# A gated window attention: w_q loaded in two pieces, wo's first piece in halves around the last values, three blocks ahead of the parts' sum

## The chip, the core and the metric

The kernel runs on one core of a Trainium2 chip. The core has a matrix engine (TensorE, PE in the profile; its weight loads are listed as PEld), a vector engine (VectorE, DVE), a scalar engine (ScalarE, ACT), GpSimd (POOL) and SyncE (SP), which here only issues DMAs. Each engine works through its own instructions in order and waits on semaphores. Sixteen DMA engines carry the transfers; every large transfer is spread over all of them. The metric is the device time of one execution in microseconds, the median of the runs shown.

## The reference

Two tokens (batch 2, one position, D = 512) are normalised and go through two branches. What is computed, cut to what matters:

```python
xn = layernorm(x)                                   # (2, 1, 512)
# A: attention, 32 query heads, 8 key/value heads of 128, over the last W = 4096 positions
q = xn @ wq                                         # wq (512, 4096)
k, v = k_cache[:, :, -W:], v_cache[:, :, -W:]       # (2, 8, 4096, 128), float32
p = softmax(q k^T * 128**-0.5);  o = p v
s = o.reshape(2, 1, 4096) @ wo                      # wo (4096, 512)
# B: a gated MLP
z = gelu(xn @ w_in)                                 # w_in (512, 1792)
z1, z2 = z[..., :896], layernorm(z[..., 896:])
y = (z1 * (w_sp * z2 + b_sp)) @ w_out               # w_out (896, 512)
out = x + s * silu(y)
```

All is float32. The data to read are some 89 MB: keys and values 33.5 MB each, wq and wo 8.4 MB each, w_in 3.7 and w_out 1.8 MB.

## The kernel before

The large loads all go through SyncE's queue, in this order: win and wout (the MLP's weights), wq in a piece of 4 MB and two of 2 MB (lines 126 to 131), and then the keys K:u and values V:u of eight units u, 4 MB each, and wo. A unit is one batch row and two key/value heads (`load`, line 146). These loads share a ring of four 4 MB slots (line 105, `slot`): win, the two halves of wq, K:0, K:1, V:0, K:2, V:1 and so on take the slots in turn, so that each load is issued when the last reader of the slot's previous content is done. For a K that reader is VectorE's transposition, for a V it is TensorE. xs, the two rows of x, comes over ScalarE's queue (line 119).

The head of the kernel normalises x (`bn_stats`, line 186), turns it (xnT), multiplies win (z, line 240), and runs the MLP between the pieces of wq; `queries(k)` (line 257) multiplies the k-th quarter of wq, and quarters 2 and 3 lie in wq's second half. The order is queries(0), queries(1), the product with wout (y), its copy, queries(2), y_sum, queries(3). Then the queries are spread into qb (`place_queries`, step q).

The rest follows ORDER (line 27), a list of steps written out by hand. Every engine issues its instructions in the order in which the steps stand there (`InOrder`, line 55). For unit u: T:u.0 to T:u.7 transpose the keys on VectorE; shares, keep and scores multiply them with the queries (TensorE, ScalarE, TensorE); rowmax, mg, shmax and bias form the maximum; exp on ScalarE; probs_t transposes the probabilities on VectorE; pv:u.0 and pv:u.1 multiply with the values; lsum, shsum and weights give the softmax denominators; evac copies the result with its weight; col and gather collect it into one of three sets: heads 0 to 3 of both batch rows (units 0, 1, 4, 5), heads 4 and 5 (units 2, 6), heads 6 and 7 (units 3, 7). `spread` (TensorE) and `place` (step oT, VectorE) bring a set into the layout in which it is multiplied with wo.

wo is 32 blocks of 128 rows: 16 for the first set, 8 each for the second and the third. `load_wo(0)` (line 508) loads the first 16 in one piece of 4 MB. `load_wo(1)` loads, into the next slot, the 8 of the second set in one piece and the 8 of the third set in pieces of 4, 2, 1 and 1. `wo_early` (line 520) multiplies 28 blocks, all but the last four: steps X:0.0 to X:0.7 (two blocks each) for the first set, Y:0.0 to Y:0.3 for the second, U:0.0 and U:0.1 for the third. Block after block goes to the next of four groups of 32 rows of one PSUM bank, `part`; step parts copies it to SBUF on ScalarE and step pz (`add_parts`, line 549) sums the four groups into the bank `so`. The last four blocks are multiplied by `wo_last` (line 538) straight into `so`, 8 multiplies each (four groups, and two passes for float32): Z:0 takes the piece of two blocks, Z:1 and Z:2 one block each. The order at the end is Z:0, pz, Z:1, Z:2. Then VectorE multiplies with the gate, adds x and the result is stored (lines 601 to 604).

PSUM banks are handed out by tag: `part` has the tag s0, that of the scores of a unit's first half; acc, the product with the values, has two banks with the tag acc.

Of the kernel before, what the change touches and what calls it, by code (L numbers as in the profile page):

```python
# [9 lines left out]
F32 = mybir.dt.float32  # L10
# [4 lines left out]
P = 128  # L15
# [28 lines left out]
scores:5.1 evac:4 col:4 rowmax:5.0  # L44
K:7 V:6 T:6.0 rowmax:5.1 mg:5 T:6.1 T:6.2 shmax:5 bias:5 T:6.3 exp:5.0 T:6.4 exp:5.1 T:6.5 probs_t:5.0 shares:6.0
keep:6.0 lsum:5 shsum:5 scores:6.0 probs_t:5.1 T:6.6 T:6.7 rowmax:6.0 pv:5.0 weights:5 shares:6.1 keep:6.1 pv:5.1
V:7 T:7.0 wo:0 scores:6.1 rowmax:6.1 T:7.1 T:7.2 mg:6 T:7.3 shmax:6 bias:6 T:7.4 evac:5 col:5 exp:6.0 exp:6.1 T:7.5
probs_t:6.0 T:7.6 T:7.7 wo:1 lsum:6 shares:7.0 keep:7.0 pv:6.0 scores:7.0 shares:7.1 rowmax:7.0 keep:7.1 shsum:6
scores:7.1 probs_t:6.1 weights:6 rowmax:7.1 mg:7 pv:6.1 evac:6 shmax:7 gather:5 col:6 bias:7 exp:7.0 gather:6 exp:7.1
probs_t:7.0 spread:0 probs_t:7.1 lsum:7 spread:1 pv:7.0 shsum:7 oT:0 weights:7 pv:7.1 X:0.6 X:0.0 oT:1 X:0.2 X:0.4  # L50
evac:7 X:0.3 col:7 X:0.7 gather:7 spread:2 X:0.5 Y:0.1 Y:0.0 Y:0.3 X:0.1 Y:0.2 oT:2 U:0.0 U:0.1 parts:0 Z:0 pz:0 Z:1 Z:2
"""


# [16 lines left out]
def kernel(  # L71
# [14 lines left out]
    pe, dve, act, sp = (InOrder(tc, e) for e in (nc.tensor, nc.vector, nc.scalar, nc.sync))  # L86
    B, _, D = x.shape
# [21 lines left out]
    ps = ctx.enter_context(tc.tile_pool(name="ps", bufs=1, space=bass.MemoryType.PSUM))  # L109

    def slot(name, *shape):
        return ring.tile([P, *shape], F32, tag="slot", name=name)

    def bank(name, *shape):
        return ps.tile([P, *shape], F32, tag="kt", name=name, bufs=2)


    xs = sb.tile([B, D], F32, tag="ss", name="xs", bufs=1)
    act.dma_start(xs, x[:, 0, :])
    win_v = w_in.rearrange("(p k) f -> p k f", p=P)  # L120
    win = slot("win", KT, F)
    sp.dma_start(win, win_v)
# [2 lines left out]
    wq_v = wq.rearrange("(p k) f -> p k f", p=P)  # L125
    wqt = []
    for a in range(0, KT, 2):
        t = slot(f"wq{a}", 2, HQ * DH)
        for k, n in ((0, 2),) if a == 0 else ((0, 1), (1, 1)):
            sp.dma_start(t[:, k : k + n], wq_v[:, a + k : a + k + n, :])  # L130
        wqt += [t[:, 0], t[:, 1]]

    wb1 = cst.tile([1, 2], F32, tag="wb1", name="wb1")
# [12 lines left out]
    def load(u, src, name):  # L146
        t = slot(f"{name}{u}", UJ, DH)
        b, v = divmod(u, HKV // 2)
        first = src[b, 2 * v, SK - W, :]
        of = bass.AP(tensor=src.tensor, offset=first.offset, ap=[[UJ * DH, P // 2], [SK * DH, 2], [1, UJ * DH]])  # L150
        sp.dma_start(t.rearrange("p j d -> p (j d)"), of)
        return t
# [73 lines left out]
    for nj in (8, 16):  # L226
# [3 lines left out]
        at = cst.tile([P, nx], F32, tag=f"at{nj}", name=f"at{nj}")  # L230
# [6 lines left out]
    pz = bank("z", 2, FH // G)  # L237
# [30 lines left out]
    u = cst.tile([P, 2, FT, B], F32, tag="u", name="u")  # L268
# [71 lines left out]
    def place_queries():  # L340
        dve.tensor_tensor(
            free_ap(qb, 16, [[REP, G], [32, NP * G], [1, REP]]), free_ap(qa, 0, [[0, G], [REP, NP * G], [1, REP]]),
            free_ap(grpm, 0, [[1, G], [0, NP * G], [0, REP]]), op=ALU.mult,
        )
# [10 lines left out]
    sets = {}  # L355
    for i, (kv, n, nj) in enumerate(SETS):
        o1 = cst.tile([P, B, 32], F32, tag=f"o1_{i}", name=f"o1_{i}")
        oT = cst.tile([P, nj, 32], F32, tag=f"oT_{i}", name=f"oT_{i}")
# [102 lines left out]
    col = {}  # L461
# [22 lines left out]
    def spread(i):  # L484
        o1, oT, nj = sets[f"oT{i}"]
        pts[i] = bank(f"oT_ps{i}", B, 32)
        pe.matmul(pts[i], perms[nj][0].rearrange("p h a x -> p (h a x)"), o1, start=True, stop=True)

    def place(i):
        _, oT, nj = sets[f"oT{i}"]  # L490
        nx = 32 // nj
        t = sb.tile([P, B, nx, nj], F32, tag="ot", name=f"ot{i}", bufs=1)
        dve.tensor_tensor(
            t, pts[i].rearrange("p b (x j) -> p b x j", x=nx), free_ap(perms[nj][1], 0, [[0, B], [1, nx], [0, nj]]),
            op=ALU.mult,
        )
        dve.tensor_reduce(
            oT[:, :, 0 : 16 * B : 16].rearrange("p j b -> p b j"), t.rearrange("p b x j -> p b j x"), axis=AX.X, op=ALU.add
        )


    wo_s = []
# [2 lines left out]
        wo_s.append(wo[r0:r1, :].rearrange("(p j) d -> p j d", j=nj))  # L505
    blocks = []

    def load_wo(n):
        t = slot(f"wo{n}", 16, D)
        a = 0  # L510
        for i in ((0,), (1, 2))[n]:
            for j, n in (((0, 16),), ((0, 8),), ((0, 4), (4, 2), (6, 1), (7, 1)))[i]:
                sp.dma_start(t[:, a : a + n, :], wo_s[i][:, j : j + n, :])
                blocks.append((t[:, a : a + n, :], sets[f"oT{i}"][1], j))
                a += n

    EARLY = 28
    done = 0
# [1 line left out]
    def wo_early(n, at):  # L520
        nonlocal done
        if done == 0:
            part.append(ps.tile([P, 512], F32, tag="s0", name="part"))
        t, oT, j = blocks[n]
        for a in range(at, at + 2):
            g = done % G
            pe.matmul(
                part[0][32 * g : 32 * g + 32, :], oT[:, j + a, :], t[:, a, :], start=(done < G), stop=(done >= EARLY - G)
            )
            done += 1  # L530

    part = []

    def copy_parts():
        parts.append(sb.tile([P, D], F32, tag="o", name="parts", bufs=1))
        act.activation(parts[0], part[0], AF.Copy)

    def wo_last(n):
        if n == 0:
            so.append(bank("so", DC))  # L540
        t, oT, j = blocks[3 + n]
        for a in range(t.shape[1]):
            for g in range(G):
                pe.matmul(
                    so[0][32 * g : 32 * g + 32, :], oT[:, j + a, :], t[:, a, g * DC : (g + 1) * DC],
                    start=(n == 0 and a == 0), stop=(j + a == oT.shape[1] - 1),
                )

    def add_parts():
        for g in range(G):  # L550
            pe.matmul(
                so[0][32 * g : 32 * g + 32, :], rowm, parts[0][:, g * DC : (g + 1) * DC], start=False, stop=False
            )

    parts, so = [], []
    STEPS = dict(
        T=turn, rowmax=row_max, mg=spread_max, shmax=share_max, bias=bias, exp=probs, probs_t=probs_t, lsum=own_sum,
        shsum=share_sum, weights=weights, shares=shares, keep=keep, scores=scores, pv=pv, evac=evacuate, col=collect,
        gather=gather,
    )  # L560

    def step(name, u, a=()):
        if name == "q":
            place_queries()
        elif name == "K":
            units[u].k = load(u, k_cache, "k")
        elif name == "V":
            units[u].v = load(u, v_cache, "v")
        elif name == "wo":
            load_wo(u)  # L570
        elif name == "spread":
            spread(u)
        elif name == "oT":
            place(u)
        elif name == "X":
            wo_early(0, 2 * a[0])
        elif name == "Y":
            wo_early(1, 2 * a[0])
        elif name == "U":
            wo_early(2, 2 * a[0])  # L580
        elif name == "Z":
            wo_last(u)
        elif name == "parts":
            copy_parts()
        elif name == "pz":
            add_parts()
        else:
            STEPS[name](units[u], *a)
# [6 lines left out]
    for line in ORDER.strip().split("\n"):  # L595
        for name in line.split():
            name, at = name.split(":")
            u, _, a = at.partition(".")
            step(name, int(u), (int(a),) if a else ())
# [33 lines left out]
```

## Time and profile before

| what | us |
|---|---|
| median of 3 runs (216.70 to 216.98) | 216.95 |
| the profiled execution | 216.95 |
| its span, first to last instruction | 215.2 |
| PE busy | 134.8 (63%) |
| DVE busy | 126.3 (59%) |
| ACT busy | 51.3 (24%) |
| DMA, mean rate over the span | 416 GB/s |

The profile is of one execution. Times in its rows are microseconds from the span's start. A row of the timeline gives start, duration, engine, line, operation, output and inputs, shapes and count; several instructions of a kind that follow each other are merged into one row with their count. In brackets stands how long the engine was idle before and what ended that. Nearly all instructions carry line 65, that of the helper that issues them, so they are told apart by the tiles' names. The row of a stretch gives its bounds, its length, the busy time and count of the engines asked for, the granted share of TensorE's clock, the busy share of the 16 DMA engines and their rate in GB/s.

### The profile page before, as it was taken

Reading aid. Unit: us, or ns where it says so; the run is one execution under the profiler, and the core shown is the slowest. Engines: PE = TensorE matmul, PEld = TensorE weight load, DVE = VectorE, ACT = ScalarE, POOL = GpSimd, SP = SyncE. Lnnn points to the kernel's source line nnn. Section 1 sums busy time; section 2 is a strip of 40 time slices with the busy share of each in tenths; the row PEclk is TensorE's granted clock in tenths of the full one; section 3 lists DMA queues with packets and bytes.
Section 4 is the critical chain, followed back from the end, with each engine's and each line's share of the span. In section 5 each row is a group of like instructions: output and inputs, shape, how many; then the busy total and the mean of one; then the engine's idle time right before and its main releaser. Section 6 shows DMA issues by size and latency. Waiting matters only on the chain.

```text
span 215.2 us, 2275 instructions
## 1 busy us (share of the span) xinstructions
PE 134.8 (63%) x872; PEld 42.8 (20%) x872; DVE 126.3 (59%) x217; ACT 51.3 (24%) x128; POOL 4.5 (2%) x17
## 2 busy tenths in 40 slices
PE   0174498305857928944890795299349618987893
PEld 0120222001112211312230231113113211232331
DVE  2604311749599599649917981994599089635111
ACT  5002402200116206023330503151251306142201
POOL 8000000000000000000000000000000000000000
PEclk9999559855599985995898599559859976996999
DMA  7999999999999999999999999999999999999990
GB/s 257 427 439 469 390 420 472 397 463 408 463 408 451 423 414 463 402 458 414 451 417 433 439 414 460 402 463 414 445 426 431 433 408 463 408 463 411 410 382 35
DMA packets 3930, 89.54 MB, mean 416 GB/s; under 512 B 446, under 2 KB 462, under 8 KB 848
## 3 DMA queue, kind: packets, MB, share of 16 engines
q1 hardware_dynamic: 3900, 89.40, 96.9%
q8 instruction: 7, 0.11, 0.2%
q14 instruction: 3, 0.02, 0.0%
q10 hardware_dynamic: 20, 0.01, 0.0%
HBM read 89.40 MB, written 0.00 MB: 416 GB/s over the span
## 4 chain that ended last, share of the span: by engine, by line
DMA 73%; DVE 13%; PE 10%; ACT 2%; SPq 1%; issue 1%; ACTq 0%
DMA k<-in_A_k_cache_dram 42%; DMA wq<-in_A_wq_dram 16%; DMA wo<-in_A_wo_dram 15%; DVE kts L65 10%; PE part L65 4%; PE sh L65 2%; PE acc L65 2%; ACT p L65 1%; DVE pT L65 1%; PE q_ps L65 1%; SPq L65 1%; DVE m L65 1%; PE s L65 1%; PE so L65 0%; DVE nb L65 0%
## 5 line engine op out<-in xcount | busy, mean ns | idle before, releaser
L65 DVE STREAM_TRANSPOSE kts<-k 128x1024 f32<-128x1024 f32 x64 | 75.5, 1218 | 33.0 <-DMA k<-in_A_k_cache_dram 33.0
L65 PE MATMUL sh<-kts,qb 128*32 128x512 f32 x256 | 43.7, 808 | 15.8 <-DVE kts L65 12.4
L65 PE MATMUL acc<-v,pT 128*32 128x512 f32 x256 | 33.6, 641 | 5.5 <-DMA v<-in_A_v_cache_dram 3.1
L65 ACT ACTIVATE p<-s,nb 128x512 f32<-128x512 f32 x32 | 22.5, 732 | 43.8 <-DVE nb L65 43.8
L65 ACT ACTIVATE ss<-sh 128x512 f32<-128x512 f32 x16 | 9.6, 597 | 62.1 <-PE sh L65 62.1
L65 PE MATMUL mo<-mg,joint 128*128 128x16 f32 x16 | 4.4, 355 | 29.2 <-DVE mg L65 29.2
L65 DVE STREAM_TRANSPOSE pT<-p 128x1024 f32<-128x1024 f32 x16 | 19.6, 1225 | 2.3 <-ACT p L65 2.2
L65 PE MATMUL s<-ss,sums 128*128 128x512 f32 x32 | 18.8, 671 | 2.3 <-ACT ss L65 2.3
L65 PEld LDWEIGHTS sh<-kts,qb 128*32 128x32 f32 x256 | 9.0, 130 | 39.1 <-issue 35.4
L65 PEld LDWEIGHTS acc<-v,pT 128*32 128x32 f32 x256 | 10.6, 142 | 29.0 <-issue 23.1
L65 DVE TENSOR_REDUCE m<-s 128x1 f32<-128x512 f32 x16 | 10.8, 673 | 5.3 <-PE s L65 5.2
L65 ACT ACTIVATE o<-acc,wd 128x128 f32<-128x128 f32 x32 | 9.1, 368 | 15.3 <-PE acc L65 15.3
L65 PE MATMUL q_ps<-wq,xnT 128*32 128x512 f32 x64 | 11.1, 789 | 2.6 <-DMA wq<-in_A_wq_dram 2.6
L65 PEld LDWEIGHTS mo<-mg,joint 128*128 128x128 f32 x16 | 3.6, 280 | 32.9 <-DVE mg L65 30.2
L65 PE MATMUL z<-win,xnT 128*32 128x448 f32 x32 | 6.1, 945 | 4.4 <-DMA win<-in_B_w_in_dram 4.4
L65 PE MATMUL part<-wo,oT 128*32 128x512 f32 x56 | 7.7, 596 | 1.0 <-DMA wo<-in_A_wo_dram 0.9
L65 PEld LDWEIGHTS s<-ss,sums 128*128 128x128 f32 x32 | 5.0, 197 | 10.8 <-issue 8.2
L65 ACT ACTIVATION_READ_ACCUMULATOR p<-s,nb 128x1 f32 x32 | 6.4, 200 | 0.0
L65 DVE STREAM_TRANSPOSE zs<-zs 128x448 f32<-128x448 f32 x1 | 0.6, 645 | 9.0 <-ACT zs L65 9.0
L65 ACT ACT_TABLE_LOAD x4 | 5.1, 1283 | 2.6 <-POOL hT L164 2.6
L65 DVE TENSOR_SCALAR gate<-ys 128x128 f32<-128x128 f32 x1 | 0.2, 226 | 8.8 <-ACT ys L65 8.8
L65 PE MATMUL col<-o,selw 128*32 128x128 f32 x64 | 4.0, 301 | 1.9 <-ACT o L65 1.9
(109 smaller groups left out, 63.9 us busy)
## 6 DMA issues: line engine op xcount, KB each, us to landing
k<-in_A_k_cache_dram SPq DMA_DIRECT2D x8, 4096.0 KB, 27.1
v<-in_A_v_cache_dram SPq DMA_DIRECT2D x8, 4096.0 KB, 31.2
wq<-in_A_wq_dram SPq DMA_DIRECT2D x1, 4096.0 KB, 24.2
wq<-in_A_wq_dram SPq DMA_DIRECT2D x2, 2048.0 KB
wo<-in_A_wo_dram SPq DMA_DIRECT2D x1, 4096.0 KB, 32.3
win<-in_B_w_in_dram SPq DMA_DIRECT2D x1, 3584.0 KB, 11.2
wo<-in_A_wo_dram SPq DMA_DIRECT2D x1, 2048.0 KB
wout<-in_B_w_out_dram SPq DMA_DIRECT2D x1, 1792.0 KB, 15.0
```

Source lines behind the costliest of these rows:

```text
L65: return self.tc.keep_in_program_order(call(*args, **kwargs))
```

## The change

Five edits go together.

1. wq's second half is loaded in one issue of 4 MB instead of two of 2 MB.
2. xs is loaded by two issues of one row instead of one issue of two rows.
3. wo's first piece (16 blocks) is loaded in two halves of 8 blocks (2 MB): the first is issued ahead of the last values V:7, the second behind them. wo's slot is thus taken ahead of that of V:7. The steps of the first set change with it: X:0.0 to X:0.3 multiply the first half, X:1.0 to X:1.3 the second. X:0.0 to X:0.3 stand ahead of pv:7.0, the product with the last values; for that gather:5, spread:0 and oT:0, which prepare the first set, move forward. X:1.0 and X:1.1 stand ahead of col:7, X:1.2 and X:1.3 behind it.
4. The third set's blocks come in pieces of 4, 3 and 1 instead of 4, 2, 1 and 1. Z:0 now multiplies three blocks, ahead of pz; Z:1 multiplies the last one; there is no Z:2.
5. `part` takes a bank of the tag acc.

The blocks, multiplies and bytes are the same in all.

```diff
--- before.py
+++ after.py
@@ ORDER @@
-V:7 T:7.0 wo:0 scores:6.1 rowmax:6.1 T:7.1 T:7.2 mg:6 T:7.3 shmax:6 bias:6 T:7.4 evac:5 col:5 exp:6.0 exp:6.1 T:7.5
-probs_t:6.0 T:7.6 T:7.7 wo:1 lsum:6 shares:7.0 keep:7.0 pv:6.0 scores:7.0 shares:7.1 rowmax:7.0 keep:7.1 shsum:6
-scores:7.1 probs_t:6.1 weights:6 rowmax:7.1 mg:7 pv:6.1 evac:6 shmax:7 gather:5 col:6 bias:7 exp:7.0 gather:6 exp:7.1
-probs_t:7.0 spread:0 probs_t:7.1 lsum:7 spread:1 pv:7.0 shsum:7 oT:0 weights:7 pv:7.1 X:0.6 X:0.0 oT:1 X:0.2 X:0.4
-evac:7 X:0.3 col:7 X:0.7 gather:7 spread:2 X:0.5 Y:0.1 Y:0.0 Y:0.3 X:0.1 Y:0.2 oT:2 U:0.0 U:0.1 parts:0 Z:0 pz:0 Z:1 Z:2
+wo:0.0 V:7 wo:0.1 T:7.0 scores:6.1 rowmax:6.1 T:7.1 T:7.2 mg:6 T:7.3 shmax:6 bias:6 T:7.4 evac:5 col:5 exp:6.0 exp:6.1
+T:7.5 gather:5 probs_t:6.0 T:7.6 T:7.7 wo:1.0 wo:2.0 wo:2.1 wo:2.2 lsum:6 shares:7.0 keep:7.0 spread:0 pv:6.0 scores:7.0
+shares:7.1 rowmax:7.0 keep:7.1 shsum:6 oT:0 scores:7.1 probs_t:6.1 weights:6 rowmax:7.1 mg:7 pv:6.1 evac:6 shmax:7 col:6
+bias:7 exp:7.0 gather:6 X:0.0 X:0.1 exp:7.1 probs_t:7.0 X:0.2 X:0.3 probs_t:7.1 lsum:7 spread:1 pv:7.0 shsum:7 weights:7
+pv:7.1 oT:1 X:1.0 evac:7 X:1.1 col:7 X:1.2 gather:7 spread:2 X:1.3 oT:2 Y:0.0 Y:0.1 Y:0.2 Y:0.3 U:0.0 U:0.1 parts:0
+Z:0 pz:0 Z:1
@@
-    act.dma_start(xs, x[:, 0, :])
+    for b in range(B):
+        act.dma_start(xs[b : b + 1, :], x[b, :, :])
@@
-        for k, n in ((0, 2),) if a == 0 else ((0, 1), (1, 1)):
-            sp.dma_start(t[:, k : k + n], wq_v[:, a + k : a + k + n, :])
+        sp.dma_start(t, wq_v[:, a : a + 2, :])
@@
-    def load_wo(n):
-        t = slot(f"wo{n}", 16, D)
-        a = 0
-        for i in ((0,), (1, 2))[n]:
-            for j, n in (((0, 16),), ((0, 8),), ((0, 4), (4, 2), (6, 1), (7, 1)))[i]:
-                sp.dma_start(t[:, a : a + n, :], wo_s[i][:, j : j + n, :])
-                blocks.append((t[:, a : a + n, :], sets[f"oT{i}"][1], j))
-                a += n
+    PIECES = (((0, 8), (8, 8)), ((0, 8),), ((0, 4), (4, 3), (7, 1)))
+    wo_t = {}
+
+    def load_wo(i, n):
+        if i < 2 and n == 0:
+            wo_t[i] = slot(f"wo{i}", 16, D)
+        t, at = (wo_t[i], 0) if i < 2 else (wo_t[1], 8)
+        j, count = PIECES[i][n]
+        sp.dma_start(t[:, at + j : at + j + count, :], wo_s[i][:, j : j + count, :])
+        blocks.append((t[:, at + j : at + j + count, :], sets[f"oT{i}"][1], j))
@@ wo_early @@
-            part.append(ps.tile([P, 512], F32, tag="s0", name="part"))
+            part.append(ps.tile([P, 512], F32, tag="acc", name="part", bufs=2))
@@ wo_last @@
-        t, oT, j = blocks[3 + n]
+        t, oT, j = blocks[4 + n]
@@ step @@
-            load_wo(u)
+            load_wo(u, a[0])
...
-            wo_early(0, 2 * a[0])
+            wo_early(u, 2 * a[0])
...
-            wo_early(1, 2 * a[0])
+            wo_early(2, 2 * a[0])
...
-            wo_early(2, 2 * a[0])
+            wo_early(3, 2 * a[0])
```

## The prediction

> **What bounds the kernel now.** First I read the page: its span and its DMA rows. The first number of the third row is the count of packets, then come MB and the share of 16 DMA engines.
>
> ```profile
> span 215.2 us, 2275 instructions
> DMA  7999999999999999999999999999999999999990
> q1 hardware_dynamic: 3900, 89.40, 96.9%
> q8 instruction: 7, 0.11, 0.2%
> ```
>
> The 16 DMA engines are full in every slice but the first and the last. One queue of loads carries 89.4 MB and takes 96.9% of the engines' time. To see whether it ever runs dry I read the rate by stretch (stretch, us, granted clock, DMA share, GB/s), SyncE's issues, and two pieces of the chain that ended last.
>
> ```profile
> 36.00:60.00 24.00, 0.64 0.99 429
> 120.00:190.00 70.00, 0.80 1.00 433
> 38.62 36.62 DMA k<-in_A_k_cache_dram
> 169.36 16.87 SPq L65 DMA_DIRECT2D wo<-in_A_wo_dram  x6
> 169.36 32.28 DMA wo<-in_A_wo_dram
> ```
>
> The rate is flat near 432 GB/s, so 4 MB take 4.19/0.432 = 9.7 us. K:2, issued at 38.62, lands 36.6 us later, that is behind almost four such pieces; the first wo piece, issued at 169.36, lands 32.3 us later. The queue is always three to four pieces deep, so a load issued a few us sooner or later moves nothing. What can move the time is the length of the stream and what follows its last byte. The end, from the timeline and from the wo tile's issues (one window each for the last two pieces):
>
> ```profile
> 209.04 0.31 PEld L65 LDWEIGHTS part<-wo,oT 128*32 128x32 f32 x8 [0.55 <-issue]
> 210.28 0.65 PE L65 MATMUL so<-wo,oT 128*32 128x128 f32 x16
> 210.35 0.60 ACT L65 ACTIVATE parts<-part 128x512 f32<-128x512 f32 x1 [8.24 <-PE part L65]
> 211.00 0.43 PE L65 MATMUL so<-parts,rowm 128*32 128x128 f32 x8
> 211.25 0.64 PE L65 MATMUL so<-wo,oT 128*32 128x128 f32 x16
> 211.96 0.29 DVE L65 TENSOR_TENSOR res<-so,gate 128x128 f32<-128x128 f32 x1 [5.70 <-PE so L65]
> L65 SPq DMA_DIRECT2D wo<-in_A_wo_dram x1: 432/432/432, 185.3 to 185.3; - x1
> DMA to landing us min/median/max: 25.5/25.5/25.5
> L65 SPq DMA_DIRECT2D wo<-in_A_wo_dram x1: 432/432/432, 185.8 to 185.8; - x1
> DMA to landing us min/median/max: 25.6/25.6/25.6
> ```
>
> The last two 256 KB pieces land at 185.3 + 25.5 = 210.8 and 185.8 + 25.6 = 211.4. TensorE's last group of 16 starts at 211.25 and ends at 211.89; its second half is the block that lands at 211.4. So two things end together: the parts' sum (copied by ScalarE until 210.95, added from 211.00) and the last landing. The sum waits for the copy, but taking the copy away alone would win next to nothing.
>
> **The change part by part.**
>
> *w_q's second half in one piece.* The same bytes in one issue. Step queries(2) now waits for all 4 MB instead of the first 2 MB.
>
> ```profile
> 36.63 1.93 PE L65 MATMUL q_ps<-wq,xnT 128*32 128x512 f32 x16 [0.63 <-DMA wq<-in_A_wq_dram]
> 41.95 1.23 DVE L65 TENSOR_TENSOR qb<-qa,grpm 128x1024 f32<-128x1024 f32 x1 [1.31 <-PE qa L65]
> 46.28 9.13 DVE L65 STREAM_TRANSPOSE kts<-k 128x1024 f32<-128x1024 f32 x8 [3.11 <-DMA k<-in_A_k_cache_dram]
> ```
>
> Its 16 multiplies (1.93 us, as the row of 36.63 has it for the next 16) and y_sum with the copy behind it (0.6 us) move from before 36.6 to behind it, so K:2's issue and qb come about 2.5 us later; qb ends at 43.2 now, then at 45.7. Behind qb on VectorE stand the first transposes, which wait for K:0 until 46.28: hidden by 0.6 us. At half clock qb would end near 47.6 and the transposes start 1.3 us late, which the three pieces queued ahead of K:3 cover. Cost 0; bounds 0 to +0.1.
>
> *xs as two rows.* One issue more on ScalarE's queue.
>
> ```profile
> 2.25 0.68 DVE L65 BATCH_NORM_STATS2 st<-xs 2x6 f32<-2x512 f32 x1
> 7.65 0.17 DVE L65 COPY xnT<-xnT_ps 128x8 f32<-128x8 f32 x1 [0.79 <-PE xnT_ps L65]
> 12.04 6.13 PE L65 MATMUL z<-win,xnT 128*32 128x448 f32 x32 [4.43 <-DMA win<-in_B_w_in_dram]
> SPq L65 <- DMA win<-in_B_w_in_dram: 8.6, 1, 8.6
> ```
>
> xnT is ready at 7.82, TensorE waits for win until 12.04: 4.2 us of cover for a second row that lands late. Beyond that, z and the waits behind it (K:1's issue) slip by the excess, into a deep queue. Cost 0. K:0's issue, which waits 8.6 us for win, waits for this second row instead (the eight completion semaphores are handed out in turn): it goes out earlier, behind 13 MB of weights. Gain 0.
>
> *wo's first piece in halves around V:7.* V:7 and wo's first half swap their waits (K:6 turned; V:5 multiplied): the two issues, the second at 169.36, stay. V:7 lands 2 MB later: 4.85 us. V:7 landed 9.7 us ahead of wo's first piece (169.36 + 32.28 = 201.65), near 192; so now near 196.8.
>
> ```profile
> 195.08 3.38 PE L65 MATMUL acc<-v,pT 128*32 128x512 f32 x16 [1.39 <-DVE pT L65]
> 198.90 1.95 PE L65 MATMUL acc<-v,pT 128*32 128x512 f32 x16
> 201.78 2.34 PE L65 MATMUL part<-wo,oT 128*32 128x512 f32 x18 [0.93 <-DMA wo<-in_A_wo_dram]
> 204.84 0.29 DVE L65 TENSOR_REDUCE o<-col 128x32 f32<-128x128 f32 x1 [4.91 <-PE part L65]
> 205.55 4.71 PE L65 MATMUL part<-wo,oT 128*32 128x512 f32 x32
> 206.60 0.19 PEld L65 LDWEIGHTS part<-wo,oT 128*32 128x32 f32 x8 [0.91 <-issue]
> ```
>
> pv:7.0 starts 1.8 us later, but at full clock (16 in 1.95 instead of 3.38 us), so pv:7.1 ends again near 200.9. Half of the X blocks are multiplied before V:7 lands. Behind 201.65 only X:1 is left: two steps of 0.43 us instead of five ahead of col:7, so the last values (204.84 now) come some 1.2 us earlier. That wins nothing: Y starts at 206.60, right behind the landing of its 2 MB (201.65 + 4.85 = 206.5), and U at 209.04 behind its own. Both landings stay; the parts are copied by 210.95 as now. Term 0.
>
> *Three blocks in one piece, multiplied ahead of the sum.* Z:0 held blocks 4 and 5 of the last set (16 multiplies at 210.28, before the sum); now it holds 4, 5 and 6 in one 768 KB piece. That ends where the 256 KB piece of block 6 ended: 210.8. Then TensorE's order is 24 multiplies, 8 for the sum, 8 for the last block. From the rows: 16 take 0.65 us with 0.27 for a single one, so each 8 occupy 0.22; the sum's 8 take 0.25 before the next group starts. 210.8 + 0.03 + 3 x 0.22 = 211.5; + 0.25 = 211.75; + 0.22 + 0.17 until the last one ends = 212.1, against 211.89. The block of 211.4 no longer waits for its landing but for TensorE. Term +0.2. Bounds: 0 (TensorE follows the last landing as now) and +0.45 (all 24 and the 8 of the sum behind 211.0).
>
> *Stream length.* Same bytes; 128 descriptors of 32 KB instead of 256 of 16 KB in w_q, the reverse in wo, one piece less at the end. The flat rate allows 0; bounds -0.1 to +0.1.
>
> Sum: 0 + 0 + 0 + 0.2 + 0 = +0.2 us. The profiled execution took 216.95 us (span 215.2 and 1.75 around it), which is also the median: **217.15 us**. A measurement here tells about 0.2% (0.43 us) from no change, so this is "same".
>
> **The rivals.** *Half clock at the end* (slower). With less left behind 201.65 the last values come at 203.6, their spread at 204.0, and X:1.3 behind it, which alone takes 1.0 us (as the step at 205.55 does, until 206.60), ends near 205.3. TensorE is then idle until Y at 206.6, beside a wait of 0.4 for the last values: some 1.65 us of idleness in a stretch of 3.4. The granted clock of this trace changes on a grid of 3.41 us; what idleness does is read from windows on that grid (PE busy, count, clock, DMA share, GB/s):
>
> ```profile
> 130.61:134.02 3.41, 1.66 (x14) 1.00 0.94 399
> 134.02:137.43 3.41, 0.00 (x0) 0.50 1.00 432
> 62.34:65.75 3.41, 1.87 (x18) 1.00 1.03 442
> 65.75:69.17 3.42, 2.47 (x22) 1.00 1.06 460
> ```
>
> A window with 1.66 us of work was followed by half clock, one with 1.87 was not; I expect 1.75. If it falls, Y's 16 take 3.4 us (the 195.08 row), until 210.0, U's 8 until 211.2, the copy until 211.9, sum and last block until 212.6: 0.7 later than 211.89, **217.65 us**. It needs a window laid over just that gap, so I give it 0.25. The Trainium skill, "TensorE: Matmul & The Clock Gate", Part 1 and "HAM oscillation", has a free-running window of 3413 ns and asks for no idle gap over about 3.4 us; by that gap rule the rival would be impossible and the sum stay 217.15. The trace agrees on the window and is stricter on the gap.
>
> *The engines' lag* (faster, or slower). The stream does not end on all engines at once (DMA share, GB/s at the end):
>
> ```profile
> 209.25:209.50 0.25, 1.00 0.64 246
> 209.50:209.75 0.25, 1.00 0.46 180
> 210.20:210.40 0.20, 1.00 0.45 174
> 210.80:211.00 0.20, 1.00 0.16 61
> ```
>
> Half of them are done by 209.5, the last at 211.0. Spread evenly, the rest of 209.25 to 211.0 (shares of 0.64 down to 0.16, in all 0.7 us of full work) would end at 210.0, 1 us sooner. The seven instruction transfers (0.2% of 16 x 215.2 = 6.9, so 1.0 us each on one engine) can set a single engine back so far. If they fall on other engines, or behind the last data, landings come up to 1.0 earlier, and I price it at half to all of that, less 0.2: **216.4 us**; it decides once the last landings come over 0.65 us earlier. The instruction stream is nearly the same, which speaks against it: 0.17. The opposite, one more on the latest engine, gives +1.0: 218.1, 0.10.
>
> *The reordering doing what its words say.* If the three blocks were done before the sum is ready, the end would follow the sum by 0.25 + 0.39: 211.64, 0.25 sooner, 216.7. That needs the 768 KB by 210.3, half a us before its bytes can be there: 0.06.
>
> **How the numbers follow.** Forecast 0.42 (217.15, own range 216.9 to 217.4), words' rival 0.06: same 0.48. Half clock 0.25 and lag grown 0.10: slower 0.35. Lag shrunk: faster 0.17. The range 216.4 to 217.9 leaves out the grown lag and half of the shrunk one.
>
> **What would show it.** The 768 KB piece landing at 210.8 and so<-wo as one group of 24 right behind it, so<-parts near 211.5 and not waiting for ScalarE, res near 212.15; V:7's multiplies near 196.9 at full clock; Y still at 206.6. A PE clock of 0.50 after 206 shows the half-clock rival; last landings away from 210.8 and 211.4 the lag. Idle DMA slices before 205 would overthrow the whole.

## The result, and the profile after

| | before | after |
|---|---|---|
| median, us (16 runs each) | 216.95 (216.65 to 217.33) | 217.41 (217.07 to 217.58) |
| profiled execution, us | 216.95 | 217.38 |
| its span, us | 215.2 | 215.5 |

The ratio is 1.0019, with a 95% interval of 1.0012 to 1.0026: 0.26 to 0.56 us slower, a loss that can be told from nothing, and about the 0.2% that the prediction called the same. Of the 0.43 us between the two profiled executions 0.3 lie inside the span, at its end, as the rows below show; the other 0.1 lies outside the span, where no row shows it.

The end of the changed kernel, first its chain of waits (start, us, what):

```profile
184.92 25.86 DMA wo<-in_A_wo_dram
210.78 0.14 issue
210.92 1.33 PE so L66 x40
212.25 0.02 issue
212.28 0.30 DVE res L66
```

Before, the chain ended with the part's multiplies, ScalarE's copy and 24 multiplies into so. Now it comes straight from a landing, that of the 768 KB piece (210.78), into 40 multiplies that run without a gap. The timeline has them one by one, with what stands before them:

```profile
206.62 1.92 PE L66 MATMUL part<-wo,oT 128*32 128x512 f32 x16 [1.49 <-DMA wo<-in_A_wo_dram]
209.07 1.07 PE L66 MATMUL part<-wo,oT 128*32 128x512 f32 x8 [0.53 <-DMA wo<-in_A_wo_dram]
210.92 0.86 PE L66 MATMUL so<-wo,oT 128*32 128x128 f32 x24 [0.78 <-DMA wo<-in_A_wo_dram]
211.57 0.43 PE L66 MATMUL so<-parts,rowm 128*32 128x128 f32 x8
211.79 0.43 PE L66 MATMUL so<-wo,oT 128*32 128x128 f32 x8
212.28 0.29 DVE L66 TENSOR_TENSOR res<-so,gate 128x128 f32<-128x128 f32 x1 [7.49 <-PE so L66]
L66 SPq DMA_DIRECT2D wo<-in_A_wo_dram x1: 432/432/432, 185.4 to 185.4; - x1
DMA to landing us min/median/max: 26.0/26.0/26.0
```

The multiplies of the steps Y and U start where they did (206.6 and 209.1). The last landing is where it was too: 185.4 + 26.0 = 211.4. The last block no longer follows it: its multiplies start at 211.79, behind the other 32, and end at 212.22 instead of 211.89. That is 0.33 us, and VectorE's first operation behind so is 0.32 later (212.28, 211.96 before).

The middle went as the prediction has it, or is hidden. The values' product and the head, from the timeline, and the rate of the long stretch in the middle (stretch, us, granted clock, DMA share, GB/s):

```profile
7.17 0.68 DVE L66 BATCH_NORM_STATS2 st<-xs 2x6 f32<-2x512 f32 x1 [4.95 <-DMA xs<-in_A_x_dram]
12.29 6.12 PE L66 MATMUL z<-win,xnT 128*32 128x448 f32 x32 [0.26 <-DVE xnT L66]
45.03 1.23 DVE L66 TENSOR_TENSOR qb<-qa,grpm 128x1024 f32<-128x1024 f32 x1 [1.31 <-PE qa L66]
46.82 9.13 DVE L66 STREAM_TRANSPOSE kts<-k 128x1024 f32<-128x1024 f32 x8 [0.57 <-DMA k<-in_A_k_cache_dram]
196.89 1.95 PE L66 MATMUL acc<-v,pT 128*32 128x512 f32 x16 [2.04 <-DMA v<-in_A_v_cache_dram]
203.01 0.29 DVE L66 TENSOR_REDUCE o<-col 128x32 f32<-128x128 f32 x1 [2.89 <-PE col L66]
120.00:190.00 70.00, 0.75 1.01 433
```

VectorE can use xs almost 5 us later (7.17, 2.25 before), and z begins 0.25 us later; qb ends at 46.26, still 0.56 before the first transposition, which waits for its keys; pv:7.0 runs at 196.9 at full clock (16 multiplies in 1.95 us). The stream carries 433 GB/s as before.

### The profile page after: what moved, and what is told of

Its sections match the earlier page's. It is cut to its first block, busy times and chain, and to the rows that moved or that the text cites. A ratio compares the mean times of both kernels' runs of the same rounds, so it can differ in the third digit from the quotient of the medians.

```text
span 215.5 us, 2275 instructions
## 1 busy us (share of the span) xinstructions
PE 134.9 (63%) x872; PEld 41.9 (19%) x872; DVE 126.0 (58%) x217; ACT 51.4 (24%) x128; POOL 4.5 (2%) x17
## 4 chain that ended last, share of the span: by engine, by line
DMA 70%; DVE 22%; PE 3%; ACT 2%; issue 1%; SPq 0%
DMA k<-in_A_k_cache_dram 53%; DVE kts L66 18%; DMA wo<-in_A_wo_dram 12%; DMA win<-in_B_w_in_dram 5%; DVE pT L66 2%; ACT p L66 2%; PE sh L66 2%; DVE m L66 1%; PE so L66 1%; DVE nb L66 1%; PE s L66 1%; SPq L66 0%; ACT ss L66 0%; DVE res L66 0%; DVE mg L66 0%
## 5 line engine op out<-in xcount | busy, mean ns | idle before, releaser
L66 PE MATMUL sh<-kts,qb 128*32 128x512 f32 x256 | 44.2, 819 | 13.2 <-DVE kts L66 9.8
L66 PE MATMUL q_ps<-wq,xnT 128*32 128x512 f32 x64 | 10.4, 794 | 4.8 <-DMA wq<-in_A_wq_dram 4.8
L66 PE MATMUL xnT_ps<-ident,xn 2*128 2x2 f32 x4 | 0.6, 252 | 11.4 <-DVE xn L66 11.4
```

The lines of the kernel that those rows point to most:

```text
L66: return self.tc.keep_in_program_order(call(*args, **kwargs))
```

## The experiments

Theory A is the prediction's: TensorE's work behind the late 768 KB piece is the loss. Theory B puts it in the head or in the later last values, theory C in the sum that stands behind three blocks. Each kernel ran eleven times beside the kernel before on the same chip (six times for the one without X:1); the ratios are to the kernel before.

| run | median, us | before beside it | ratio (95%) |
|---|---|---|---|
| changed, pieces 4, 2, 1, 1 again | 217.05 | 216.86 | 1.0007 (0.9998 to 1.0015) |
| before, pieces 4, 3, 1 alone | 217.20 | 216.86 | 1.0016 (1.0007 to 1.0025) |
| before, w_q and xs alone | 216.96 | 216.86 | 0.9999 (0.9991 to 1.0008) |
| before, halves around V:7 alone | 217.06 | 216.86 | 1.0009 (1.0000 to 1.0017) |
| before, order at the end alone | 216.85 | 216.85 | 1.0000 (0.9991 to 1.0009) |
| changed, sum ahead of Z:0 | 217.21 | 216.85 | 1.0018 (1.0009 to 1.0026) |
| changed, without X:1 | 217.68 | 216.85 | 1.0041 (1.0025 to 1.0056) |
| before, x added in so, ahead of U | 216.67 | 216.85 | 0.9995 (0.9986 to 1.0004) |
| before, x added in so, ahead of X | 216.50 | 216.79 | 0.9985 (0.9976 to 0.9994) |
| the same, three blocks ahead of the sum | 216.52 | 216.79 | 0.9984 (0.9975 to 0.9993) |
| before, halves both behind V:7 | 217.00 | 216.87 | 1.0009 (1.0000 to 1.0018) |

**The parts one by one.** The changed kernel with its last pieces undone:

```diff
-    PIECES = (((0, 8), (8, 8)), ((0, 8),), ((0, 4), (4, 3), (7, 1)))
+    PIECES = (((0, 8), (8, 8)), ((0, 8),), ((0, 4), (4, 2), (6, 1), (7, 1)))
-wo:2.0 wo:2.1 wo:2.2
+wo:2.0 wo:2.1 wo:2.2 wo:2.3
...
-Z:0 pz:0 Z:1
+Z:0 pz:0 Z:1 Z:2
```

> The changed kernel with the third set's pieces again 4, 2, 1 and 1 blocks and the end again Z:0 (two blocks), the sum, Z:1, Z:2. Theory A (the whole loss is TensorE's work behind the 768 KB piece): the end follows the last landing again, within 0.1 us of the kernel before (216.95). Theory B (the loss lies in the head, in w_q's one piece and xs in two rows, or in the later last values): stays near the changed kernel, 217.3 to 217.4.

The kernel before with those pieces alone:

```diff
-            for j, n in (((0, 16),), ((0, 8),), ((0, 4), (4, 2), (6, 1), (7, 1)))[i]:
+            for j, n in (((0, 16),), ((0, 8),), ((0, 4), (4, 3), (7, 1)))[i]:
-parts:0 Z:0 pz:0 Z:1 Z:2
+parts:0 Z:0 pz:0 Z:1
```

> The kernel before with the third set in pieces of 4, 3 and 1 alone, all three blocks of the middle piece multiplied ahead of the sum. Theory A: 0.3 to 0.45 us slower than before, 217.25 to 217.4, the last TensorE group ending near 212.2. Theory B: no change, 216.95.

The kernel before with w_q's second half in one piece and xs in two rows:

```diff
-    act.dma_start(xs, x[:, 0, :])
+    for b in range(B):
+        act.dma_start(xs[b : b + 1, :], x[b, :, :])
-        for k, n in ((0, 2),) if a == 0 else ((0, 1), (1, 1)):
-            sp.dma_start(t[:, k : k + n], wq_v[:, a + k : a + k + n, :])
+        sp.dma_start(t, wq_v[:, a : a + 2, :])
```

> The kernel before with w_q's second half in one piece and xs in two rows alone. Theory A: no change (within 0.1 us of 216.95), though queries(2), the gate and qb come 2 to 3 us later and the second row of xs lands near 11 us. Theory B: 0.3 to 0.45 us slower.

And the kernel before with wo's first piece in halves around the last values, that is the changed kernel with the two edits above undone:

```diff
-    for b in range(B):
-        act.dma_start(xs[b : b + 1, :], x[b, :, :])
+    act.dma_start(xs, x[:, 0, :])
-        sp.dma_start(t, wq_v[:, a : a + 2, :])
+        for k, n in ((0, 2),) if a == 0 else ((0, 1), (1, 1)):
+            sp.dma_start(t[:, k : k + n], wq_v[:, a + k : a + k + n, :])
-    PIECES = (((0, 8), (8, 8)), ((0, 8),), ((0, 4), (4, 3), (7, 1)))
+    PIECES = (((0, 8), (8, 8)), ((0, 8),), ((0, 4), (4, 2), (6, 1), (7, 1)))
...
```

> The kernel before with wo's first piece in halves around the last values alone (with the steps that follow from it, and the sum's bank). Theory A: no change (within 0.1 us of 216.95): Y and U start behind their landings, at 206.6 and 209.05. Theory B: 0.3 to 0.45 us slower if the later last values cost.

The pieces alone cost 0.16%, most of what the whole change costs; the head costs nothing that can be measured. In the profile of the pieces alone the chain ends as in the changed kernel, a landing and 40 multiplies without a gap:

```profile
184.51 25.93 DMA wo<-in_A_wo_dram
210.44 0.14 issue
210.58 1.33 PE so L65 x40
```

This execution's stream ended some 0.3 us sooner than that of the changed kernel, so its absolute times are to be read against its own landings. The last piece landed at 185.0 + 26.1 = 211.1 and the last multiply ended at 211.9: 0.8 us behind it, where the kernel before has 211.9 - 211.4 = 0.5. The same difference, the end of the last group less the last landing, is 0.8 us in all three traces with the 768 KB piece at full clock (the changed kernel, this one, and the one with the sum first, below). It is 0.5 in all traces with the small pieces, but for the first run with x added in so, below. Undoing the pieces wins most of the loss back (1.0007). The halves alone read 1.0009, at the edge of what can be told. Both of these were expected within 0.1 us of the kernel before and came out 0.2 above it by the medians; to that below.

**Order or piece.** The kernel before with its own pieces, but three blocks ahead of the sum:

```diff
-parts:0 Z:0 pz:0 Z:1 Z:2
+parts:0 Z:0 Z:1 pz:0 Z:2
```

> The kernel before with its pieces of 4, 2, 1 and 1, but three blocks ahead of the sum (Z:0, Z:1, sum, Z:2). Theory A (the cost is that 24 multiplies wait together for one late 768 KB piece): no change, within 0.1 us of the kernel before, since Z:0 is done by 210.9 and Z:1 needs 0.22 us behind 210.8. Theory C (the cost is the sum standing behind three blocks): 0.2 to 0.35 us slower.

The changed kernel with the sum first:

```diff
-Z:0 pz:0 Z:1
+pz:0 Z:0 Z:1
     def add_parts():
+        so.append(bank("so", DC))
...
-rowm, parts[0][:, g * DC : (g + 1) * DC], start=False, stop=False
+rowm, parts[0][:, g * DC : (g + 1) * DC], start=True, stop=False
```

> The changed kernel with the sum ahead of Z:0 instead of behind it. Theory A: the work behind 210.8 is the same 40 multiplies on TensorE in another order, so the time stays at that of the changed kernel, 0.4 to 0.5 us over before, last group ending near 212.2. Theory C: 0.2 us or more is won back.

Theory C falls: the same order without the 768 KB piece costs nothing (1.0000), and with the piece the other order wins nothing that can be told (1.0018 beside the 1.0019 of the changed kernel). With small pieces two blocks are multiplied before the third lands; the timeline of the order alone:

```profile
210.05 0.98 PE L65 MATMUL so<-wo,oT 128*32 128x128 f32 x24
210.84 0.40 PE L65 MATMUL so<-parts,rowm 128*32 128x128 f32 x8
211.24 0.43 PE L65 MATMUL so<-wo,oT 128*32 128x128 f32 x8
```

The 24 multiplies start at 210.05, the sum at 210.84, and the last eight right behind the landing of the last piece (185.5 + 25.7 = 211.2): the end follows that landing again. With the sum first in the changed kernel, 40 multiplies stand behind 210.8 all the same, for the sum itself waits for ScalarE's copy of the parts, which ends then:

```profile
210.82 0.42 PE L66 MATMUL so<-parts,rowm 128*32 128x128 f32 x8 [0.77 <-ACT parts L66]
211.06 1.06 PE L66 MATMUL so<-wo,oT 128*32 128x128 f32 x32
```

**The half clock.** The changed kernel without X:1.0 to X:1.3 (8 of wo's 32 blocks are left out), which makes TensorE idle ahead of Y:

```diff
-EARLY = 28
+EARLY = 20
-pv:7.1 oT:1 X:1.0 evac:7 X:1.1 col:7 X:1.2 gather:7 spread:2 X:1.3 oT:2
+pv:7.1 oT:1 evac:7 col:7 gather:7 spread:2 oT:2
```

> The changed kernel without the multiplies X:1.0 to X:1.3 (8 of wo's 32 blocks are left out of the output). TensorE is then idle from about 203.5 until Y at 206.6. The half-clock rival: the granted clock falls to 0.50 during Y or U, the sum comes 0.4 to 0.8 us later, and the time is 0.3 to 0.8 us above that of the changed kernel, although less is computed. If the clock does not matter there: the time of the changed kernel, 0.4 to 0.5 us over before, or less.

Less work, and no faster: 1.0041 (1.0025 to 1.0056) beside the 1.0019 (1.0012 to 1.0026) of the changed kernel. The profiled execution is the slowest of the six (218.25). Its windows on the clock's grid (stretch, us, PE busy, count, granted clock, DMA share, GB/s), its timeline, and then the windows of the changed kernel:

```profile
202.09:205.50 3.41, 0.86 (x10) 1.00 0.96 408
205.50:208.92 3.42, 2.55 (x13) 0.50 1.00 418
208.92:212.33 3.41, 3.41 (x33) 0.50 0.28 109
206.37 5.35 PE L66 MATMUL part<-wo,oT 128*32 128x512 f32 x24 [2.94 <-DMA wo<-in_A_wo_dram]
212.76 0.41 PE L66 MATMUL so<-wo,oT 128*32 128x128 f32 x8
```

```profile
202.51:205.92 3.41, 2.62 (x22) 1.00 0.95 404
205.92:209.34 3.42, 2.19 (x20) 1.00 0.98 408
209.34:212.75 3.41, 2.10 (x48) 1.00 0.20 76
```

A window with 0.86 us of work was followed by two at half clock; Y and U took 5.35 us, and the last group ended at 213.17, 0.95 behind that of the changed kernel. The six runs lie between 217.16 and 218.25 us, wider than any other kernel's here. That fits a grid that falls differently over the gap from run to run, but only one of the six has a trace, so the spread's cause is argued. In the changed kernel's one trace no window near the end fell below 2.1 us of work, and its 16 runs lie within 0.51 us.

**What stands behind the last landing.** If theory A holds, anything taken away behind the last landing is won one to one. VectorE's addition of x was taken off the end: x divided by the gate is put into so by TensorE, and the multiplication with the gate gives it back.

```diff
+    off = cst.tile([P, 1], F32, tag="off", name="off")
+    dve.tensor_reduce(off, ident[:, 0 : P : P // (G * B)], axis=AX.X, op=ALU.add)
+    dve.tensor_scalar(off, off, -1.0, 1.0, op0=ALU.mult, op1=ALU.add)
+    xg = cst.tile([P, DC], F32, tag="xg", name="xg")
+    dve.tensor_scalar(xg, gate, off, None, op0=ALU.add)
+    dve.reciprocal(xg, xg)
+    dve.tensor_mul(xg, xg, x4)
...
+    def add_x():
+        so.append(bank("so", DC))
+        for g in range(G):
+            pe.matmul(so[0][32 * g : 32 * g + 32, :], ident[:, 32 * g : 32 * g + 32], xg, start=True, stop=False)
...
-Y:0.2 oT:2 U:0.0
+Y:0.2 R:0 oT:2 U:0.0
...
-    dve.tensor_add(res, res, x4)
```

> The kernel before, with x added on TensorE: x divided by the gate is put into the bank so ahead of U (8 multiplies in an idle stretch, the division on VectorE near 40 us), so the last of VectorE's two operations behind so falls away (0.29 us and 0.03 between them). Theory A (what stands behind the last landing counts one to one, the rest is hidden): 0.3 us faster than before, near 216.6. If the end were held by something else: no change; if the 1.6 us more on VectorE near 40 us were not hidden: slower.

Only 0.18 us by the medians, and no gain beyond the interval. The timeline, of the slowest of the eleven executions (216.90), shows what can have eaten it:

```profile
209.28 0.42 PE L65 MATMUL so<-xg,ident 128*32 128x128 f32 x4
209.50 1.06 PE L65 MATMUL part<-wo,oT 128*32 128x512 f32 x6
211.30 0.43 PE L65 MATMUL so<-parts,rowm 128*32 128x128 f32 x8 [0.31 <-ACT parts L65]
```

x's multiplies mingle with U, U ends 0.3 us later (0.07 of that because it also starts later in this execution), and the sum starts at 211.30 instead of 211.00. So they were put where TensorE is idle anyway, ahead of X:0.6:

```diff
-pv:7.1 X:0.6 X:0.0
+pv:7.1 R:0 X:0.6 X:0.0
-Y:0.2 R:0 oT:2 U:0.0
+Y:0.2 oT:2 U:0.0
```

> x in the bank so as in the run before, but its 8 multiplies stand ahead of X:0.6, where TensorE is idle until wo's first piece lands, instead of ahead of U, where they pushed the sum from 211.0 to 211.3. Theory A (what stands behind the last landing counts one to one): 0.3 us faster than the kernel before, 216.55, the sum back at 211.0 and one VectorE operation behind so. If the gain stays at 0.18 us or less, something else than the pushed sum ate it.

And the same with Z:0, Z:1, the sum, Z:2:

> The same with three blocks ahead of the sum (Z:0, Z:1, sum, Z:2), in pieces of 4, 2, 1 and 1. Theory A: the same as without that order, within 0.1 us, 216.5 to 216.55; together the fastest kernel. Theory C (a sum behind three blocks costs): 0.2 us slower than without.

They come out at 0.9985 and 0.9984: 0.3 us faster than the kernel before, which agrees with the 0.32 us that were taken away (0.29 for the operation and 0.03 ahead of it). In the first one's timeline the sum no longer waits for U (the copy starts at 210.03, the last piece lands at 185.4 + 25.7 = 211.1):

```profile
210.68 0.42 PE L65 MATMUL so<-parts,rowm 128*32 128x128 f32 x8 [0.15 <-ACT parts L65]
210.92 0.66 PE L65 MATMUL so<-wo,oT 128*32 128x128 f32 x16
211.64 0.29 DVE L65 TENSOR_TENSOR res<-so,gate 128x128 f32<-128x128 f32 x1 [5.76 <-PE so L65]
```

The last group ends at 211.58, 0.5 us behind the last landing, as in the kernel before. This version divides by the gate, so it is good only where no element of the gate is zero.

**The halves.** wo's first piece in two issues, both behind V:7 as before:

```diff
-            for j, n in (((0, 16),), ((0, 8),), ((0, 4), (4, 2), (6, 1), (7, 1)))[i]:
+            for j, n in (((0, 8), (8, 8)), ((0, 8),), ((0, 4), (4, 2), (6, 1), (7, 1)))[i]:
-            wo_early(0, 2 * a[0])
+            wo_early(a[0] // 4, 2 * (a[0] % 4))
...
```

> The kernel before with wo's first piece loaded in two issues of 8 blocks, both still behind V:7, steps otherwise unchanged. If the 0.1 to 0.2 us that the runs with halves around V:7 showed are the stream's (256 descriptors of 16 KB instead of 128 of 32 KB), this one shows them too: 216.95 to 217.0 beside 216.8. If they come from the later last values, it shows none. If they are noise, none either.

1.0009, as with the halves around V:7, so the later last values are not the cause. The landings and TensorE are not either, as far as the traces go: the last piece lands at 185.5 + 25.8 = 211.3 here and at 185.8 + 25.6 = 211.4 with the halves around V:7, and the last group ends 0.5 us behind it in both, as in the kernel before.

What differs stands behind the store of the result. At the end SyncE waits for the semaphores of the DMAs, one after the other. In the rows below EVENT_SEMAPHORE is such a wait; count, shortest, median and longest duration in ns, and first and last start in us follow. The first row is of the kernel before, the second of this run, each with the waits that were open or still to come when the result landed:

```profile
L628 SPq EVENT_SEMAPHORE x1: 28/28/28, 214.3 to 214.3; - x1
L628 SPq EVENT_SEMAPHORE x4: 28/28/882, 213.3 to 214.4; - x4
```

In the kernel before, the result's landing ends the last of these waits. Here it ends an earlier one, that of 882 ns, and three more of some 0.06 us each follow. The three kernels that have the halves and still the four last pieces (the changed kernel with its pieces back, the halves around V:7, and this one) all end so: from VectorE's first operation behind so to the end of the span they take 3.35 to 3.39 us. The kernel before, the changed kernel and the other four that have the same two operations there and as many DMAs take 3.16 to 3.26 us. The difference is some 0.15 us, and the medians of the three are 0.13 to 0.20 above the kernel before.

The three issue 33 DMAs, the kernel before and the changed kernel 32; with the pieces alone it is 31, and one wait follows the result's landing. So the cost of the halves, which the intervals leave between 0 and 0.18%, is most likely that of one DMA more at the program's end, and the changed kernel does not pay it. Why the number of DMAs moves the result's wait in that row of waits is not shown.

## Why the prediction was right, point by point

*The bound.* Right. The stream ran at 433 GB/s in both and ended at 211.4 in both profiles; all that was gained or lost in the span lay behind it. The run that takes 0.32 us away there wins 0.3.

*w_q's second half.* Right: queries(2) moved behind the landing, qb ended at 46.26 (45.7 was worked out) and the first transposition still waits for its keys (46.82, 0.5 us later than before, with their landing). No cost (0.9999).

*xs in two rows.* Right in cost, nearly wrong in cover. xs was complete so late that the 4.2 us of cover were used up and z slipped by 0.25 us, which the time does not show. What it says of K:0 was wrong: its issue was said to go out earlier, and the changed kernel still issues it at 11.97, behind win's landing.

*The halves.* Right in all places that it names (pv:7.0 at 196.9, Y at 206.6, U at 209.07), except that the two issues do not stay: V:7 went out at 172.36, not 169.36, with no effect, for the queue is deep. The last values came at 203.0 (203.6 expected).

*Three blocks in one piece.* The mechanism was right to the group: 24, 8 and 8 multiplies without a gap, from the landing of 210.8, with the last landing no longer the bound. Its size was short: +0.2 was forecast, +0.33 measured in the trace. The 0.03 us between landing and first multiply was 0.14, and the last group took 0.43 us from its start where 0.39 was taken; the sum's eight gave 0.03 back (0.22 for 0.25). Both count in full, since nothing else is left to hide them. Both could be read before: in the kernel before, wo's first piece lands at 201.65 and is used at 201.78, and the row of 211.00 has 0.43 for eight multiplies.

*Stream length.* Right: taken as 0 within 0.1, and the last landing is at 211.4 in both profiles. The halves' possible cost is at the program's end, and the changed kernel, with as many DMAs as the kernel before, has none of it.

*The total.* 217.41 lies 0.01 above the forecast's own range of 216.9 to 217.4, and the loss of 0.46 by the medians is more than twice the +0.2; only the wide range, drawn for the rivals, holds it with room. The profiled executions differ by 0.43: what was said of the three blocks makes up 0.33, and the 0.1 outside the span stays open.

*The rivals.* Half clock at the end is real, as the run without X:1 shows, with about 0.95 us in its trace (0.7 was worked out). In the changed kernel's trace X:1.2 filled the wait for the last values, so that TensorE was idle from 205.13 to 206.62 alone. However the grid falls, a window there holds at least 3.41 - 1.49 = 1.9 us of work, where 1.75 was expected, and the two that it touched held 2.6 and 2.2. The line that 1.66 and 1.87 seemed to draw is not sharp: in the thirteen traces a window of 1.77 us was followed by half clock (130.83 to 134.24 in the changed kernel) and one of 1.59 was not (199.75 to 203.17 with both halves behind V:7), but none of 1.79 or more was. So 1.9 is above all that fell, though not by much. The Trainium skill's "TensorE: Matmul & The Clock Gate" asks for no gap over about 3.4 us; in the run without X:1 a gap of 2.9 us with little work ahead of it was enough, so here the work in a window tells more than the length of one gap. The lag of the DMA engines did not move between the two profiles. The reordering did what its words say only with pieces small enough (the run with the order alone), and was worth nothing there.

## What to carry to other kernels

Where a stream of loads is the bound, look for the work that stands behind its last bytes, and cut the last pieces so that the work of all but the very last is done when that one lands: joining a 512 KB and a 256 KB piece saved a transfer and held back 24 multiplies. Here what was added or taken away behind the last landing counted in full, and what moved ahead of it did not count; extra work put there belongs in an idle stretch, not just ahead of the chain's end. When a small difference has no place in the stream, look at the program's closing waits too. That two waits end together, so that removing the one that the chain names wins nothing, is argued alone: no run takes the copy of the parts away and leaves the rest.

## What the runs showed that was not expected

Two transfers of one 2 KB row each, issued on ScalarE's queue one behind the other, held VectorE until 7.17 us (7.15 in the run with w_q and xs alone, where 11 was expected); both rows in one issue were used at 2.25. The Trainium skill, "DMA: Bandwidth & Descriptors", section on why a DMA increments its semaphore by 16 and not by 1, says that a DMA issued by ScalarE or SyncE that uses fewer than the core's 16 engines runs on the lowest-numbered ones. That a row ran on few engines and queued there behind the first bulk loads would fit, but no row here shows the engine.

The first multiply behind the 768 KB piece began 0.14 us after its landing (210.78 to 210.92 in the chain, and again 210.44 to 210.58 in the run with the pieces alone), not the 0.03 that had been taken.
